# Another form of the feature map in a linear-attention block: three passes instead of four or five

## The chip, the cores and the metric

The kernel runs on one core of one Trainium2 chip. The time is the device time in microseconds (us), a median over several executions. The engines are named as the profile names them: PE (TensorE, matmuls), PEld (its weight loads), DVE (VectorE), ACT (ScalarE), POOL (GpSimd) and SP (SyncE, which here only issues DMAs). Each engine works through its own instructions in the order in which the program gives them; semaphores hold an instruction until what it needs is there. An instruction that waits holds up everything behind it on its engine.

## What is computed

One block of a network: layer norm, linear attention, a SwiGLU feed-forward network on the same normalised input, and a gated residual. There are 2048 tokens of width 1024, 32 heads of width 32, and a hidden width of 3584. All inputs are bfloat16.

```python
xn = _layernorm(x)
qkv = (xn @ wqkv) ...            # q, k, v per head
phi = lambda t: jnp.where(t > 0, t + 1, jnp.exp(t)) + 1e-6
pq, pk = phi(q), phi(k)
kv  = einsum("bhsd,bhse->bhde", pk, v)
z   = einsum("bhsd->bhd", pk)
num = einsum("bhqd,bhde->bhqe", pq, kv)
den = einsum("bhqd,bhd->bhq", pq, z)[..., None] + 1e-6
s   = (num / den) @ wo
g   = silu((silu(xn @ w_gate) * (xn @ w_up)) @ w_down)
out = x + s * g
```

The change concerns `phi`, the feature map, alone.

## The kernel before

**Phase 1, to about 128 us.** The 2048 tokens are 16 tiles of 128. For each tile `i` the kernel normalises the tile on DVE (L447, L448, L485), transposes it, and multiplies it by the K and V weights in four units of 512 columns (`c` = 0 to 3): eight matmuls each into a PSUM tile `kv_ps` (L528), of which there are three. Units 0 and 1 are K: `emit_Bev` sends them through the feature map into `pk_sb`, in bfloat16. Units 2 and 3 are V: ACT copies them to `v_sb` (L543). A tile later `emit_C` (L550) adds pk'v and the sum of pk to an accumulator `kvz`, which stays in PSUM.

**The Q projection, about 128 to 215 us.** The tokens are now four blocks `b` of 512. `emit_Q(b, g)` multiplies 128 columns (group `g` of 8) of Wq by a block: eight matmuls into a PSUM tile `q_ps` (L183), out of five such buffers, then the feature map into `pqT`. When `kvz` is complete, DVE masks it into `KVZ` (L662, L664). For each token tile of a block whose eight groups are done, `emit_ND` multiplies `pqT` by `KVZ`: eight matmuls into `nd` (L717). DVE then empties `nd`: it adds the epsilon to the denominators (L721), takes their reciprocals (L725) and writes the quotients to `o_blk` (L729, three instructions). There is one `nd` buffer. SP issues a DMA that transposes `o_blk` into `oT` (L738), and `emit_S` multiplies that by Wo (L748); ACT scales and stores the result (L751).

`run` (L865) sets the order: it takes a list of units, and after certain ones (`at`) puts in an `nd` item. For block 1 the list is eight Q units with an `nd` item of block 0 after every second; for blocks 2 and 3, Q units and S units alternate and an `nd` item follows every third unit. For blocks 1 and 2 an `nd` item also carries one step of weight preparation (`prep_step`).

**The feature map, `emit_phi`,** has three forms, all for 128 partitions by 512 columns:

- `in_place=False` (K of tiles 0 to 8): ACT Exp from PSUM into `e_t` (L154); ACT Relu from PSUM into `r_t` in SBUF (L161); DVE adds eps to `r_t` (L162); DVE takes min(e, 1) + r (L163). PSUM is free after the Relu.
- `in_place=True` (K of tiles 9 to 15, and groups 0, 1, 2, 4, 6 of Q block 0): ACT Exp (L154); DVE takes max(t, 0) + eps in PSUM (L157); DVE takes min(e, 1) + r with r in PSUM (L163).
- `act=True` (groups 3, 5, 7 of Q block 0 and all of blocks 1 to 3): ACT Relu(-t) into `e_t` (L148), ACT Exp(-that) in place (L149), ACT Relu(t) in PSUM (L150), then DVE adds the two and eps (L151). The DVE instruction isn't put in at once: it goes to the list `phi_late`, and `phi_flush` puts it in at the end of the step in `run`, that is behind the DVE work of an `nd` item that stands beside it.

`e_t` and `r_t` are float32, two buffers each.

**Beside all this** runs the preparation of the feed-forward weights: SP loads a weight tile, ACT sums its squares (L260), PE and DVE turn that into a power of two (L264, L269, L272, L273), DVE scales the tile in place (L283, 128 by 2048 bfloat16 in SBUF), POOL makes four difference tiles (L295 to L298), and the result is stored. From tile 8 of phase 1 on this goes on almost without a break. Before the attention's last stage POOL also makes sixteen difference tiles of Wo (L762). From about 246 us on the feed-forward network runs, in which PE is busy to the end.

Of the kernel before, what the change touches and what calls it, by code (L numbers as in the profile page):

```python
# [9 lines left out]
ACT = mybir.ActivationFunctionType  # L10
ALU = mybir.AluOpType
FP32 = mybir.dt.float32
BF16 = mybir.dt.bfloat16
# [8 lines left out]
def kernel(  # L22
# [11 lines left out]
    nc = tc.nc  # L34
    P = 128
# [10 lines left out]
    TB = min(512, S)  # L46
    NB = S // TB
    TPB = TB // P
    CW = min(512, D)
# [9 lines left out]
    EPS = 1e-6  # L59
# [58 lines left out]
    def xn_ap(dcs, tok):  # L118
        b = tok.start // TB
        return xn_blk_tiles[b][:, dcs, tok.start - b * TB:tok.stop - b * TB]  # L120
# [20 lines left out]
    def phi_flush():  # L141
        while phi_late:
            phi_late.pop(0)()

    def emit_phi(work, t_ps, dst, W, in_place=False, act=False):
        e_t = work.tile([P, W], FP32, name="e_t", tag="e_t")
        if act:
            nc.scalar.activation(out=e_t[:], in_=t_ps, func=ACT.Relu, scale=-1.0)  # L148
            nc.scalar.activation(out=e_t[:], in_=e_t[:], func=ACT.Exp, scale=-1.0)  # L149
            nc.scalar.activation(out=t_ps, in_=t_ps, func=ACT.Relu)  # L150
            phi_late.append(lambda: nc.vector.scalar_tensor_tensor(out=dst, in0=e_t[:], scalar=EPS, in1=t_ps,  # L151
                                                                   op0=ALU.add, op1=ALU.add))
            return
        nc.scalar.activation(out=e_t[:], in_=t_ps, func=ACT.Exp)  # L154
        if in_place:
            r = t_ps
            nc.vector.tensor_scalar(out=r, in0=t_ps, scalar1=0.0, scalar2=EPS, op0=ALU.max, op1=ALU.add)  # L157
        else:
            r_t = work.tile([P, W], FP32, name="r_t", tag="r_t")
            r = r_t[:]  # L160
            nc.scalar.activation(out=r, in_=t_ps, func=ACT.Relu)  # L161
            nc.vector.tensor_scalar(out=r, in0=r, scalar1=EPS, scalar2=None, op0=ALU.add)  # L162
        nc.vector.scalar_tensor_tensor(out=dst, in0=e_t[:], scalar=1.0, in1=r,  # L163
                                       op0=ALU.min, op1=ALU.add)


    blk12_es = ExitStack()
    blk12 = blk12_es.enter_context(tc.tile_pool(name="blk12", bufs=2, side="right", reuse_waits="tile"))
    phiw = p12.enter_context(tc.tile_pool(name="phiw", bufs=2, reuse_waits="tile"))
# [3 lines left out]
    def pqT_of(b):  # L173
        if b not in pqT_tiles:
            pqT_tiles[b] = blk12.tile([P, G, TB], BF16, name="pqT", tag="pqT")
        return pqT_tiles[b]

    def emit_Q(b, g, act=None):
        pqT = pqT_of(b)
        btok = slice(b * TB, (b + 1) * TB)  # L180
        q_ps = ps2.tile([P, TB], FP32, name="q_ps", tag="B2")
        for dc in range(DC):
            nc.tensor.matmul(q_ps[:], lhsT=wq_sb[:, dc, g * P:(g + 1) * P], rhs=xn_ap(dc, btok),  # L183
                             start=(dc == 0), stop=(dc == DC - 1))
        emit_phi(phiw, q_ps[:], pqT[:, g, :], TB, in_place=True, act=b > 0 if act is None else act)

    NPASS = NB // 2
    passes = list(range(NPASS - 1, -1, -1))
# [158 lines left out]
    def prep(n):  # L347
        for _ in range(n):
            prep_step()
# [13 lines left out]
    with ExitStack() as p1:  # L363
        wpool = p1.enter_context(tc.tile_pool(name="p1w", bufs=1, reuse_waits="tile"))
        work = p1.enter_context(tc.tile_pool(name="p1work", bufs=2, reuse_waits="tile"))
# [167 lines left out]
        def emit_Bev(i, c):  # L533
            kv_ps = kv_banks.pop((i, c))
            if i not in pkv_tiles:
                pk_sb = work.tile([P, D], BF16, name="pk_sb", tag="pk_sb")
                pkv_tiles[i] = (pk_sb, v_bufs[i % 2])
            pk_sb, v_sb = pkv_tiles[i]
            if c < NCC:
                emit_phi(phiw, kv_ps[:], pk_sb[:, c * CW:(c + 1) * CW], CW, in_place=i >= 9)  # L540
            else:
                vc = c - NCC
                nc.scalar.copy(out=v_sb[:, vc * GPC:(vc + 1) * GPC, 0:P],  # L543
                               in_=kv_ps[:].rearrange("p (g c) -> p g c", c=P))
# [29 lines left out]
        emit_TR(1)  # L574
        ln_pre(2)
        emit_Bev(0, 0)
        emit_Bmm(1, 0)
        emit_Bmm(0, 1)
        emit_Bev(1, 0)
        emit_N(2)  # L580
        emit_Bev(0, 1)
        emit_Bmm(1, 1)
        emit_Bmm(0, 2)
# [71 lines left out]
        ps2 = p12.enter_context(tc.tile_pool(name="ps2", bufs=5, space=PSUM, reuse_waits="tile"))  # L655
        stat_ps[0] = lambda: ps2.tile([P, 1], FP32, name="st_ps2", tag="B2")[:]
        emit_Q(0, 0)
        emit_C(NT - 1)
        for j in range(NJ):
# [3 lines left out]
                                    in1=mask[:, None, :].to_broadcast([P, ng, P]), op=ALU.mult)  # L663
            nc.vector.tensor_tensor(out=KVZ[:, g0:g0 + ng, P:P + HPG],  # L664
                                    in0=kvz_ps[:, j, 0:ng, P:P + 1].to_broadcast([P, ng, HPG]),
                                    in1=sel[:, None, :].to_broadcast([P, ng, HPG]), op=ALU.mult)
        for g in range(1, G):
            emit_Q(0, g, act=g in (3,5,7))
            if g in (2, 5):
                prep(1)  # L670
            phi_flush()
# [24 lines left out]
    with ExitStack() as p2:  # L696
        otp = p2.enter_context(tc.tile_pool(name="p2oT", bufs=2, reuse_waits="tile"))
        work = p2.enter_context(tc.tile_pool(name="p2work", bufs=4, reuse_waits="tile"))
# [137 lines left out]
        def q_item(b, g):  # L836
            return lambda: emit_Q(b, g)
# [597 lines left out]
```

## Time and profile before

| | |
|---|---|
| median of three runs | 758.13 us (757.99 to 758.14) |
| span of the profiled execution | 756.7 us |
| DVE L151, 27 times, 674 to 689 ns | Q, last step of the `act` form |
| DVE L157, 14 times on K and 5 on Q, 685 to 700 ns | max(t, 0) + eps in PSUM |
| DVE L162, 18 times, 373 to 454 ns | r + eps, float32 in SBUF |
| DVE L163, 37 times, 686 to 694 ns | min(e, 1) + r |
| ACT L148, L149, L150, 27 times each | medians 597, 630, 579 ns |
| ACT L154, 32 times on K and 5 on Q | medians 597 and 589 ns |
| ACT L161, 18 times | median 592 ns |
| DVE L283, 35 times, 747 to 3672 ns | median 755 ns |

The profile is of one execution. Its page gives each engine's busy time, the chain of work that ended last, and groups of equal instructions; the trace behind it can be asked for the order in time, for the waits, and for busy times by stretch. "Idle before" is the time that an engine stood still ahead of an instruction, and the releaser is what ended it. A time line gives the start in us from the span's beginning, the duration in us, engine, line and operation, what it writes and reads, and how many instructions are merged into the row.

### The profile page before, as it was taken

How to read it: one execution, taken by the hardware profiler on the slowest of the kernel's cores; microseconds unless marked ns; L12 is line 12 of the kernel's file. 1: busy time of each engine (PE TensorE's matmuls, PEld its weight loads, DVE VectorE, ACT ScalarE, POOL GpSimd, SP SyncE). 2: the span in 40 equal slices, each digit the busy share in tenths (PEclk: the TensorE clock that was granted, in tenths of full speed). 3: DMA queues.
4: the chain of work that ended last, by engine and by line, in shares of the span. 5: the costliest groups of instructions: out<-in, count | busy, mean ns of one | idle time of the engine just before them, and what ended most of it. 6: DMA issues, size and time to landing. Idle time of an engine off the chain costs nothing.

```text
span 756.7 us, 10426 instructions
## 1 busy us (share of the span) xinstructions
PE 746.6 (99%) x3662; PEld 349.0 (46%) x3731; DVE 558.5 (74%) x1031; ACT 376.3 (50%) x526; POOL 278.4 (37%) x352
## 2 busy tenths in 40 slices
PE   8999999999999999999999999999999999999997
PEld 4544544454454444444444444444444444444443
DVE  6687787896697788888889775368676777787335
ACT  5677776889956565666659311132322223211122
POOL 2444799998540276868585000100000000200000
PEclk9999999999999999999999999999999999999999
DMA  9968799879679668878799236398644445530824
GB/s 316 295 149 146 223 334 300 302 137 307 201 180 298 229 217 292 309 268 312 278 329 408 86 121 239 124 377 321 229 174 167 167 168 173 180 133 15 283 83 135
DMA packets 105845, 170.30 MB, mean 225 GB/s; under 512 B 34816, under 2 KB 82176, under 8 KB 95168
## 3 DMA queue, kind: packets, MB, share of 16 engines
q1 hardware_dynamic: 100144, 144.99, 59.3%
q0 software_dynamic: 4208, 22.15, 7.5%
q10 hardware_dynamic: 1440, 2.49, 0.9%
q8 instruction: 29, 0.48, 0.3%
q14 instruction: 24, 0.20, 0.1%
HBM read 111.67 MB, written 50.59 MB: 214 GB/s over the span
## 4 chain that ended last, share of the span: by engine, by line
PE 97%; DVE 1%; ACT 1%; issue 1%; ACTq 0%; DVEq 0%
PE zw L939 26%; PE kv_ps L528 15%; PE xb L939 13%; PE dzw L1124 12%; PE yb L939 6%; PE q_ps L183 6%; PE dx L1124 6%; PE dy L1124 3%; PE fx L790 3%; PE s_ps L748 2%; PE kvz L550 1%; PE nd L717 1%; PE df L1124 1%; PE warm_ps L564 1%; DVE w_sb L283 0%
## 5 line engine op out<-in xcount | busy, mean ns | idle before, releaser
L939 PEld LDWEIGHTS <-w_sb 128*128 128x128 f16 (+1 forms) x1568 | 152.1, 98 | 182.7
L939 PE MATMUL xb<-xnT,w_sb 128*128 128x512 bf16 x420 | 113.3, 379 | 1.5
L528 PE MATMUL kv_ps<-wkv_sb,xnT 128*128 128x512 bf16 x499 | 112.9, 379 | 1.1 <-DVE xnT L515 0.3
L939 PE MATMUL zw<-xnT,w_sb 128*128 128x512 bf16 x448 | 105.8, 379 | 0.0
L939 PE MATMUL zw<-S,w_sb 128*128 128x512 f16 x448 | 105.8, 379 | 0.0
L295 POOL TENSOR_TENSOR w_sb<-w_sb 128x512 f16<-128x512 bf16 x42 | 50.2, 1195 | 95.7 <-DVE w_sb L283 51.3
L260 ACT ACTIVATE w_sb<-w_sb 128x2048 bf16<-128x2048 bf16 x42 | 79.9, 1902 | 4.4 <-DMA w_sb<-in_B_w_up_dram 4.4
L1124 PE MATMUL dx<-w_sb,hT 128*128 128x512 bf16 x202 | 76.6, 379 | 0.3
L528 PEld LDWEIGHTS <-xnT 128*128 128x128 bf16 x512 | 48.4, 98 | 55.9 <-ACT xnT L517 0.8
L1124 PEld LDWEIGHTS <-hT 128*128 128x128 bf16 (+1 forms) x462 | 44.7, 98 | 52.4
L183 PE MATMUL q_ps<-xnT,wq_sb 128*128 128x512 bf16 x249 | 58.0, 379 | 0.4
L1015 ACT ACTIVATE sg<-cg 128x1024 bf16<-128x1024 f32 x28 | 29.6, 1057 | 57.4 <-DVE cg L1008 57.4
L939 PE MATMUL yb<-S,w_sb 128*128 128x512 f16 x224 | 57.4, 378 | 0.1
L1124 PE MATMUL dzw<-w_sb,hT 128*128 128x512 f16 (+1 forms) x190 | 57.0, 379 | 0.0
L1008 DVE SCALAR_TENSOR_TENSOR cg<-zw,rc_all,s 128x1024 f32<-128x1024 f32 x28 | 35.9, 1284 | 25.5 <-PE zw L939 13.8
L967 DVE SCALAR_TENSOR_TENSOR s<-yb,rc_all,s 128x512 f32<-128x512 f32 x42 | 31.5, 749 | 28.1 <-ACT s L966 28.1
L296 POOL TENSOR_TENSOR w_sb<-w_sb 128x512 f16<-128x512 bf16 x42 | 50.5, 1201 | 3.3
L1064 POOL TENSOR_TENSOR hs<-hT 128x512 f16<-128x512 bf16 x2 | 2.5, 1250 | 132.6 <-ACT sg L1015 132.6
L298 POOL TENSOR_TENSOR w_sb<-w_sb 128x512 f16<-128x512 bf16 x42 | 50.2, 1196 | 0.0
L297 POOL TENSOR_TENSOR w_sb<-w_sb 128x512 f16<-128x512 bf16 x42 | 50.2, 1195 | 0.0
L1098 POOL DMA_DIRECT2D out_dram<-io x16 | 8.7, 542 | 101.9 <-DVE io L1097 101.6
L966 ACT ACTIVATE s<-xb,rcl 128x512 f32<-128x512 f32 x14 | 9.6, 687 | 65.3 <-PE xb L939 65.3
(179 smaller groups left out, 1187.4 us busy)
## 6 DMA issues: line engine op xcount, KB each, us to landing
w_sb<-pk_g SPq DMA_DIRECT2D x27, 1024.0 KB, 6.3
pk_g<-w_sb SPq DMA_DIRECT2D x14, 1024.0 KB, 5.0
w_sb<-wd SPq DMA_DIRECT2D x14, 1024.0 KB, 6.0
w_sb<-pk_u SPq DMA_DIRECT2D x14, 1024.0 KB, 5.0
pk_u<-w_sb POOLq DMA_DIRECT2D x13, 1024.0 KB, 5.3
w_sb<-wd SPq DMA_DIRECT2D x14, 768.0 KB, 4.8
w_sb<-in_B_w_gate_dram SPq DMA_DIRECT2D x14, 512.0 KB, 6.7
w_sb<-in_B_w_down_dram SPq DMA_DIRECT2D x28, 256.0 KB, 4.9
```

The source lines that it names most:

```text
L183: nc.tensor.matmul(q_ps[:], lhsT=wq_sb[:, dc, g * P:(g + 1) * P], rhs=xn_ap(dc, btok), start=(dc == 0), stop=(dc == DC - 1))
L260: nc.scalar.activation(out=junk, in_=raw_view(key, t), func=ACT.Square, accum_out=asum[:])
L295: nc.gpsimd.tensor_tensor(out=T1, in0=b12, in1=b11, op=ALU.subtract)
L296: nc.gpsimd.tensor_tensor(out=T2, in0=b22, in1=T1, op=ALU.subtract)
L297: nc.gpsimd.tensor_tensor(out=T3, in0=b22, in1=b12, op=ALU.subtract)
L298: nc.gpsimd.tensor_tensor(out=T4, in0=b21, in1=T2, op=ALU.subtract)
L528: mm = nc.tensor.matmul(kv_ps[:], lhsT=xn_ap(dc, tok), rhs=wkv_sb[:, dc, c * CW:(c + 1) * CW], start=(dc == 0), stop=(dc == DC - 1))
L939: mm = nc.tensor.matmul(out, lhsT=lhs(k), rhs=rhs(k), start=(first and k == 0), stop=(k == HK - 1), skip_group_check=True)
L967: nc.vector.scalar_tensor_tensor(out=s2[:], in0=y_[:], scalar=rc, in1=s1[:], op0=ALU.mult, op1=ALU.add)
L1008: nc.vector.scalar_tensor_tensor(out=d12, in0=zw[:], scalar=rc, in1=s2[:, None, :].to_broadcast([P, 2, TB]), op0=ALU.mult, op1=ALU.add)
L1015: nc.scalar.activation(out=sg[:, 1:3, :], in_=cf[:], func=ACT.Silu)
L1124: nc.tensor.matmul(out, lhsT=lhs, rhs=rhs, start=first, stop=lastk, skip_group_check=True)
```

## The change

`emit_phi` is rewritten with the identity phi(t) = max(t + 1 + eps, min(exp t, 1) + eps): for t > 0 the first is larger, for t < 0 the second. It is one Exp on ACT from PSUM into `e_t`, now bfloat16; a clip on DVE in SBUF, in place, min(e, 1) + eps; and one DVE operation that reads PSUM and `e_t` and writes the result. `emit_Q` no longer chooses the `act` form, and K no longer chooses by tile. All 64 feature maps (32 of K, 32 of Q) take the same three steps, and both DVE steps of Q are now put in at once, inside `emit_Q`; `phi_late` stays empty. The `act` form remains in the code without being called.

```diff
-    def emit_phi(work, t_ps, dst, W, in_place=False, act=False):
-        e_t = work.tile([P, W], FP32, name="e_t", tag="e_t")
+    def emit_phi(work, t_ps, dst, W, act=False):
+        e_t = work.tile([P, W], FP32 if act else BF16, name="e_t", tag="e_t")
         if act:
...
         nc.scalar.activation(out=e_t[:], in_=t_ps, func=ACT.Exp)
-        if in_place:
-            r = t_ps
-            nc.vector.tensor_scalar(out=r, in0=t_ps, scalar1=0.0, scalar2=EPS, op0=ALU.max, op1=ALU.add)
-        else:
-            r_t = work.tile([P, W], FP32, name="r_t", tag="r_t")
-            r = r_t[:]
-            nc.scalar.activation(out=r, in_=t_ps, func=ACT.Relu)
-            nc.vector.tensor_scalar(out=r, in0=r, scalar1=EPS, scalar2=None, op0=ALU.add)
-        nc.vector.scalar_tensor_tensor(out=dst, in0=e_t[:], scalar=1.0, in1=r,
-                                       op0=ALU.min, op1=ALU.add)
-
+        nc.vector.tensor_scalar(out=e_t[:], in0=e_t[:], scalar1=1.0, scalar2=EPS, op0=ALU.min, op1=ALU.add)
+        nc.vector.scalar_tensor_tensor(out=dst, in0=t_ps, scalar=1.0 + EPS, in1=e_t[:], op0=ALU.add, op1=ALU.max)
...
-    def emit_Q(b, g, act=None):
+    def emit_Q(b, g, act=False):
...
-        emit_phi(phiw, q_ps[:], pqT[:, g, :], TB, in_place=True, act=b > 0 if act is None else act)
+        emit_phi(phiw, q_ps[:], pqT[:, g, :], TB, act=act)
...
-                emit_phi(phiw, kv_ps[:], pk_sb[:, c * CW:(c + 1) * CW], CW, in_place=i >= 9)
+                emit_phi(phiw, kv_ps[:], pk_sb[:, c * CW:(c + 1) * CW], CW)
...
-            emit_Q(0, g, act=g in (3,5,7))
+            emit_Q(0, g)
```

## The prediction

> **What bounds the kernel now.** I read the page's busy shares and its chain first.
>
> ```profile
> span 756.7 us, 10426 instructions
> PE 746.6 (99%) x3662; PEld 349.0 (46%) x3731; DVE 558.5 (74%) x1031; ACT 376.3 (50%) x526; POOL 278.4 (37%) x352
> PE 97%; DVE 1%; ACT 1%; issue 1%; ACTq 0%; DVEq 0%
> ```
>
> TensorE sets the end: 99% busy, 97% of the chain. ACT and DVE time counts only where PE waits for it. So I took the stretches of the feature map one by one (columns: stretch and length, then busy time of PE, PEld, DVE, ACT, POOL, then clock and DMA).
>
> ```profile
> 90.00:100.00 10.00, 9.95 (x57) 4.80 (x57) 8.27 (x15) 7.55 (x10) 9.84 (x9) 1.00 1.05 377
> ...
> 145.00:162.00 17.00, 16.85 (x106) 8.71 (x107) 14.06 (x35) 15.64 (x29) 16.92 (x16) 1.00 0.59 142
> 161.00:184.00 23.00, 22.57 (x131) 11.26 (x133) 20.13 (x47) 20.05 (x31) 20.09 (x19) 1.00 0.98 245
> ```
>
> The reader is to see three things: PE already loses nearly nothing here (0.15 us of 17); ACT is the fullest helper in 145 to 162; and POOL is busy without a break. Next, PE's order in time in the Q projection of block 1, where an nd group follows every second Q:
>
> ```profile
> 149.82 0.64 PE L717 MATMUL nd<-KVZ,pqT 128*128 128x132 bf16 x8
> 150.31 3.61 PE L183 MATMUL q_ps<-xnT,wq_sb 128*128 128x512 bf16 x16
> 153.76 0.63 PE L717 MATMUL nd<-KVZ,pqT 128*128 128x132 bf16 x8
> ...
> 157.68 0.63 PE L717 MATMUL nd<-KVZ,pqT 128*128 128x132 bf16 x8
> ```
>
> A pair (two Qs and one nd) takes PE 3.94 us (149.82 to 153.76, to 157.68). There is one nd buffer, so the next nd can't start until DVE has emptied the last one (L721, L725, L729). DVE's order in time:
>
> ```profile
> 154.01 0.69 DVE L151 SCALAR_TENSOR_TENSOR pqT<-e_t,q_ps 128x512 bf16<-128x512 f32 x1 [0.32 <-ACT q_ps L150]
> 154.61 0.37 DVE L721 TENSOR_SCALAR rden<-nd,rc_all 128x24 f32<-128x24 f32 x2
> 155.02 0.35 DVE L725 RECIPROCAL rden<-rden 128x32 f32<-128x32 f32 x1
> 155.41 1.35 DVE L729 TENSOR_TENSOR o_blk<-nd,rden 128x384 bf16<-128x384 f32 x3
> 156.68 0.68 DVE L151 SCALAR_TENSOR_TENSOR pqT<-e_t,q_ps 128x512 bf16<-128x512 f32 x1
> ```
>
> Emptying nd takes 156.68 - 154.61 = 2.07 us; with two L151 of 0.68 a pair costs DVE 3.43 of the 3.94 us.
>
> Last, from the time line of all engines, DVE's two-byte work in SBUF beside POOL:
>
> ```profile
> 137.13 1.73 DVE L283 TENSOR_SCALAR w_sb<-w_sb,cs_all 128x2048 bf16<-128x2048 bf16 x1
> 137.15 1.15 POOL L296 TENSOR_TENSOR w_sb<-w_sb 128x512 f16<-128x512 bf16 x1
> ...
> 138.26 1.60 POOL L297 TENSOR_TENSOR w_sb<-w_sb 128x512 f16<-128x512 bf16 x1
> ...
> 163.76 4.50 POOL L762 TENSOR_TENSOR To_sb<-wo_sb,To_sb 128x512 f16<-128x512 bf16 x4
> ...
> 165.13 3.67 DVE L283 TENSOR_SCALAR w_sb<-w_sb,cs_all 128x2048 bf16<-128x2048 bf16 x1
> ```
>
> Alone L283 takes 0.75 us. At 137.13 it took 1.73: it ended 0.55 us after L296 did, and the POOL operation behind it stretched from 1.15 to 1.60. At 165.13 it took 3.67 and ended 0.54 us after POOL's whole run (163.76 + 4.50). So such a DVE operation waits for POOL's running one and holds off the next. DVE operations that read PSUM show nothing of this: L151 stays at 674 to 689 ns throughout.
>
> **The change, part by part.** *ACT.* 18 Relus (L161, 0.592 us) go, 10.7 us; of 27 Q tiles two of three ACT passes go (L149 0.630, L150 0.579), 32.6 us. PE waited for ACT once in this region, 0.32 us at 173.22 with 0.39 more for its weight load, so about 0.4 comes back. One Exp into bf16 I leave at its 0.597 (the bf16 cast from PSUM, L543, is 0.586).
>
> *The clip, new on DVE, 64 times.* No such row exists. Nearest: L162 (512 wide, f32, SBUF, constants) 0.373 to 0.454; L485 at 512 columns bf16 0.410; L283 cut to 512 by L485's slope (0.545 at 1024, 0.410 at 512: 0.135 per 512), 0.754 - 3 x 0.135 = 0.35. Low end: L283 pro rata, 0.19. High end: L162's 0.45 plus a whole POOL operation of 1.15, 1.6. I take 0.35 alone, being bf16 in SBUF like L283, plus what the port adds.
>
> *The pass from PSUM* stays at L151's and L163's 0.68 to 0.69. For K tiles DVE gives up L162 (0.422) or L157 (0.696), for five Q tiles of block 0 L157 (0.694), so 18 tiles save 0.07, 19 save 0.35, and 27 Q tiles pay 0.35 more: 9.5 - 1.3 - 6.7 = +1.5 us before any wait. Spread evenly this would vanish in DVE's idle time; it isn't spread evenly.
>
> *The step that moves.* L151 of a Q used to be held back until after the nd work issued beside it. Now clip and pass stand ahead of that nd's L721, L725 and L729. If a clip waits, the whole emptying of nd waits behind it, and for that PE's next nd and the transposes into oT that SP issues.
>
> *Block 1 priced.* DVE per pair: 3.43 + 2 x 0.35 = 4.13 alone, 0.19 over PE's 3.94. POOL has no gap from 150.41 to 168.26, so each clip ends at a POOL boundary, and the pair becomes a whole number of POOL operations of 1.115 us (4.46 for four). Three (3.35) are fewer than the work; four are 4.46, plus two clips that each push POOL back by a quarter of 0.45 (0.11): 4.68. Four pairs ran from 145.61 to 161.62, 16.01 us: 4 x 4.68 - 16.0 = +2.7. Ends: with 0.19 per clip and no wait a pair is 3.81, hidden, 0; with 1.6 it is 6.63, +10.5.
>
> *Rest.* The period 161.62 to 167.30 still lies beside that POOL run with two clips: another +0.7. K tiles from 9 on and Q of block 0 (19 passes, POOL 98% busy) turn 1.38 us into 1.04 plus a wait of about 0.5 (22 L283 before 250 us average 1.223 against 0.754, 0.47 more): +0.16 each, 3 us more in some 60 us with 10 idle; through the three kv_ps banks I allow +0.5 (0 to 2). Blocks 2 and 3 after 176, where POOL has gaps: +0.3. POOL's own delay, 0.11 per clip, is covered: its last preparation ends at 212.8, phase 3 begins near 246.
>
> Sum: 2.7 + 0.7 + 0.5 + 0.3 - 0.4 = +3.8. From phase 3 on PE is full, and nothing there absorbs it. Profiled span 756.7 + 3.8 = 760.5; the runs' median lies 1.4 above that span, so 761.9, given as 762.0.
>
> *Two rules of the Trainium skill against the rows.* "SBUF — State Buffer" (SBUF: two separate sides) says the port pair that VectorE and GpSimd share is an exclusive lock held for a whole instruction. The rows at 137 agree; the one at 165.13 doesn't: two boundaries, at 166.0 and 167.1, went by without L283 getting in. By the rule a clip waits at most one operation, as I priced it; by that row up to four, which is the third rival below. "VectorE: DVE Perf Modes" (The TRN2 errata) gives 58 + FD/4 cycles at 0.96 GHz, 0.19 us for this clip as an estimate; by it alone a pair is 3.82 and block 1 costs nothing until the port adds 0.06 per clip.
>
> **The rivals.** *Hidden, no difference.* A clip this short slips in, or comes at 0.19 to 0.35: a pair is 3.8 to 4.13, 0 to +0.8 us in block 1, less 0.4 returned: 757.7 to 758.5. For: 2.9 idle us in 145 to 162 against 8 x 0.35 = 2.8. Against: POOL fills that stretch.
>
> *ACT was the limit, faster.* DVE's idle time before L151 ended with L150 (12.9 us in 10 waits), and ACT is 15.64 of 17. If the clip is 0.25 or less with its wait (break-even (3.94 - 3.43)/2), what remains is PE's lost time, at most some 2 us between 10 and 246: 756.1 to 757.7. Against: PE doesn't show more to give back.
>
> *Shut out.* As at 165.13, no clip enters POOL's sixteen operations (150.41 to 168.26). DVE then stands from about 151, PE stops at the second next nd, near 154, until 168.5: +14, 772. Against: at 137 and elsewhere the next boundary sufficed, and every entry breaks POOL's run anew.
>
> **How the numbers follow.** DVE paced by POOL's boundaries 66%, 759.7 to 768.5, likeliest 762.0; hidden 17%; ACT the limit 8%, of which 6 fall below 756.6; shut out 9%. This kernel's measurement tells 0.2% (1.5 us) from no change. Slower: 66 + 9 = 75%; within: 17 + 2 = 19%; faster: 6%. The range 757.2 to 768.5 holds the first two cases whole; the upper end is +10.4, the block 1 bound.
>
> **What would show it.** Right: the clips on DVE last 0.3 to 0.4 before 80 us and 0.6 or more between 90 and 168; nd groups in block 1 lie about 4.7 apart; PE's busy time falls short there by some 3 us; the first zw matmul is 4 us later; ACT is 43 us lighter to no gain. Wrong: clips of 0.35 amid a busy POOL, nd groups still 3.94 apart, or a PE wait that now ends with ACT or a K bank.

## The result, and the profile after

The changed kernel takes 763.23 us (762.96 to 763.48, four runs) against 758.13 us (four runs): ratio 1.0066, 95% interval 1.0051 to 1.0080. It is slower by 5.1 us. The profiled spans, 756.7 and 761.7 us, differ by 5.0.

The page after, with the lines that answer to those shown of before:

```profile
span 761.7 us, 10409 instructions
PE 746.9 (98%) x3662; PEld 348.5 (46%) x3731; DVE 567.5 (75%) x1058; ACT 339.0 (45%) x454; POOL 272.9 (36%) x352
PE 90%; DVE 5%; DMA 2%; issue 1%; ACT 1%; SPq 0%; POOL 0%; DVEq 0%; POOLq 0%; ACTq 0%
```

PE's busy time hardly moves (746.6 to 746.9), so PE does the same work and the five microseconds are time in which it waits. DVE's share of the chain goes from 1% to 5%. ACT is 37.3 us lighter, and the kernel is slower all the same. PE's waits after (who waited for whom: us in total, times, longest):

```profile
PE nd L708 <- DVE pqT L156: 1.7, 3, 0.9
PE nd L708 <- DVE o_blk L720: 1.7, 3, 0.8
```

Both stand at the nd groups: either the last `pqT` is late, or DVE hasn't emptied the one nd buffer. The busy times of the stretch around block 1 (columns as in the prediction: stretch and length, then PE, PEld, DVE, ACT, POOL, clock and DMA):

```profile
145.00:166.00 21.00, 17.59 (x102) 8.34 (x103) 20.38 (x45) 5.97 (x11) 20.92 (x19) 1.00 0.46 121
```

PE stands 3.4 of 21 us here, where before it lost 0.15 of 17. DVE is busy 20.38 of 21 us and POOL 20.92; ACT is busy 6. The time line of the changed kernel shows how one pair runs:

```profile
152.19 0.64 PE L708 MATMUL nd<-KVZ,pqT 128*128 128x132 bf16 x8 [0.77 <-DVE o_blk L720]
...
155.97 4.58 POOL L753 TENSOR_TENSOR To_sb<-wo_sb,To_sb 128x512 f16<-128x512 bf16 x4
...
156.59 0.68 DVE L155 TENSOR_SCALAR e_t<-e_t 128x512 bf16<-128x512 bf16 x1
...
156.73 0.64 PE L708 MATMUL nd<-KVZ,pqT 128*128 128x132 bf16 x8 [0.45 <-DVE o_blk L720]
...
157.91 0.52 DVE L155 TENSOR_SCALAR e_t<-e_t 128x512 bf16<-128x512 bf16 x1
...
159.07 0.37 DVE L712 TENSOR_SCALAR rden<-nd,rc_all 128x24 f32<-128x24 f32 x2
...
161.27 0.64 PE L708 MATMUL nd<-KVZ,pqT 128*128 128x132 bf16 x8 [0.45 <-DVE o_blk L720]
```

The nd groups are 4.54 us apart (152.19, 156.73, 161.27), where they were 3.94. POOL's four operations take 4.58, and the next four start 4.54 after these: a pair is exactly as long as four POOL operations. The two clips (L155) take 0.68 and 0.52. Elsewhere a clip can be shorter, or longer still (minimum, median, maximum in ns over all 64):

```profile
L155 DVE TENSOR_SCALAR e_t<-e_t x64: 241/416/1240, 12.2 to 218.3; 128x512 bf16<-128x512 bf16 x64
```

By stretch, from the clips' own records: 0.29 on average before 78 us, where POOL has only short operations; 0.80 from 78 to 128; 0.67 from 128 to 150; 0.60 beside POOL's Wo operations. A clip that meets a running POOL operation ends some 0.15 us after that operation does: at 156.59 it ended at 157.27, POOL's operation at 157.11. The POOL operation behind it lasts 1.20 instead of 1.15. Every clip that meets an operation of the weight preparation or of Wo ends so, and none waits for a second operation.

Where the 5.0 us arise, from the starts of PE's groups before and after: the first nd group comes 0.3 later (145.61, 145.90); the first pair after it takes 6.29 instead of 4.21 (+2.1); the next three 13.74 instead of 11.80 (+1.9); up to the Wo stage another 0.5 is added, with a wait of 0.8 inside the nd group that starts at 218.20. Phase 3 then starts at 249.25 instead of 244.43, another 0.2 is lost at its second group, and all of that reaches the end. The first pair, before (it ends at 149.82, shown in the prediction):

```profile
145.61 0.72 PE L717 MATMUL nd<-KVZ,pqT 128*128 128x132 bf16 x8
```

and after, with the late clips of block 0 that it waits for, beside POOL's weight preparation:

```profile
144.04 1.60 POOL L288 TENSOR_TENSOR w_sb<-w_sb 128x512 f16<-128x512 bf16 x1
144.55 1.24 DVE L155 TENSOR_SCALAR e_t<-e_t 128x512 bf16<-128x512 bf16 x1
...
145.90 0.51 PE L708 MATMUL nd<-KVZ,pqT 128*128 128x132 bf16 x6
146.43 0.52 DVE L155 TENSOR_SCALAR e_t<-e_t 128x512 bf16<-128x512 bf16 x1
...
146.57 0.23 PE L708 MATMUL nd<-KVZ,pqT 128*128 128x132 bf16 x1 [0.16 <-DVE pqT L156]
...
147.73 0.23 PE L708 MATMUL nd<-KVZ,pqT 128*128 128x132 bf16 x1 [0.93 <-DVE pqT L156]
```

The group ends at 147.96 instead of some 146.5, 1.4 late; the second group then comes another 0.9 late, waiting for `o_blk` (152.19, above).

### The profile page after: what moved, and what is told of

Its sections match the earlier page's. It is cut to its first block, busy times and chain, and to the rows that moved or that the text cites. A ratio compares the mean times of both kernels' runs of the same rounds, so it can differ in the third digit from the quotient of the medians.

```text
span 761.7 us, 10409 instructions
## 1 busy us (share of the span) xinstructions
PE 746.9 (98%) x3662; PEld 348.5 (46%) x3731; DVE 567.5 (75%) x1058; ACT 339.0 (45%) x454; POOL 272.9 (36%) x352
## 4 chain that ended last, share of the span: by engine, by line
PE 90%; DVE 5%; DMA 2%; issue 1%; ACT 1%; SPq 0%; POOL 0%; DVEq 0%; POOLq 0%; ACTq 0%
PE zw L930 25%; PE kv_ps L519 13%; PE xb L930 13%; PE dzw L1115 12%; PE yb L930 6%; PE dx L1115 6%; PE dy L1115 3%; PE fx L781 3%; PE q_ps L174 3%; PE s_ps L739 3%; DVE e_t L155 1%; DVE pqT L156 1%; DMA wkv_sb<-in_A_wqkv_dram 1%; DVE o_blk L720 1%; PE kvz L541 1%
## 5 line engine op out<-in xcount | busy, mean ns | idle before, releaser
L155 DVE TENSOR_SCALAR e_t<-e_t 128x512 bf16<-128x512 bf16 x64 | 32.9, 514 | 24.5 <-ACT e_t L154 24.5
```

The costliest lines, as they stand in the source:

```text
L155: nc.vector.tensor_scalar(out=e_t[:], in0=e_t[:], scalar1=1.0, scalar2=EPS, op0=ALU.min, op1=ALU.add)
```

## The experiments

The port theory: the clip works wholly in SBUF, so it waits for POOL's running operation, as L283 did at 137.13 in the kernel before; beside an unbroken POOL, that paces DVE and through the nd buffer PE.

**Q of blocks 1 to 3 in the old form.** `emit_phi_old` is `emit_phi` of the kernel before.

```diff
...
-        emit_phi(phiw, q_ps[:], pqT[:, g, :], TB, act=act)
+        if b > 0:
+            emit_phi_old(phiw, q_ps[:], pqT[:, g, :], TB, act=True)
+        else:
+            emit_phi(phiw, q_ps[:], pqT[:, g, :], TB)
```

> The changed kernel, with Q of blocks 1 to 3 in the old form (three ACT passes, one DVE pass held back); K and Q of block 0 keep the new one. Port theory (the clip in SBUF waits for POOL's running operation, and beside POOL's long run that paces the nd groups of block 1): the loss near 146 to 166 us goes, 758.0 to 758.8 us; nd groups 3.94 us apart. Rival, the K tiles carry the loss (three kv_ps banks freed later): 761 or more.

Measured: 759.34 us, ratio 1.0017 (1.0008 to 1.0026). After the first pair the nd groups are 3.92 to 3.95 apart again, as expected, and 3.9 us of the 5.1 are gone. This edit takes out the clips and the moved step together; later runs part them. The time is 0.5 above the expected span, because the first pair still takes 5.37: PE waits 1.4 us inside the first nd group for the last groups of block 0, whose clips stand beside POOL's weight preparation.

**K in the old forms.**

```diff
...
-                emit_phi(phiw, kv_ps[:], pk_sb[:, c * CW:(c + 1) * CW], CW)
+                emit_phi_old(phiw, kv_ps[:], pk_sb[:, c * CW:(c + 1) * CW], CW, in_place=i >= 9)
```

> The changed kernel, with K in the two old forms; all of Q keeps the new one. Port theory: nearly all of the loss stays, 762.4 to 763.4 us, nd groups of block 1 4.5 to 4.6 apart. Rival, K carries it: 760 or less.

Measured: 762.91 us, ratio 1.0064 (1.0049 to 1.0079), nd groups 4.55, 4.55 and 4.66 apart. So the loss stays without K's clips. The 0.3 us that this run is faster are not clear of the noise: the first nd group starts 0.36 earlier here (145.54, 145.90), and kernels whose code is the same up to that group start it up to 0.27 apart. But the one wait for a K bank in the changed kernel's trace (0.4 at 81 us) is gone here.

**The DVE steps of Q held back,** in blocks 1 to 3.

```diff
...
-        nc.vector.tensor_scalar(out=e_t[:], in0=e_t[:], scalar1=1.0, scalar2=EPS, op0=ALU.min, op1=ALU.add)
-        nc.vector.scalar_tensor_tensor(out=dst, in0=t_ps, scalar=1.0 + EPS, in1=e_t[:], op0=ALU.add, op1=ALU.max)
+        def two():
             nc.vector.tensor_scalar(out=e_t[:], in0=e_t[:], scalar1=1.0, scalar2=EPS, op0=ALU.min, op1=ALU.add)
             nc.vector.scalar_tensor_tensor(out=dst, in0=t_ps, scalar=1.0 + EPS, in1=e_t[:], op0=ALU.add, op1=ALU.max)
+        if late:
+            phi_late.append(two)
+        else:
+            two()
...
-        emit_phi(phiw, q_ps[:], pqT[:, g, :], TB, act=act)
+        emit_phi(phiw, q_ps[:], pqT[:, g, :], TB, act=act, late=b > 0)
```

> The changed kernel, with both DVE steps of Q in blocks 1 to 3 held back behind the nd work issued beside them, as the old form did. Port theory: two clips per pair still end at POOL boundaries, so nd groups stay 4.5 to 4.6 us apart and the time 762.3 to 763.4 us. Rival, the order (the emptying of nd starts too late because clip and pass stand ahead of it): groups back to 3.94, 760 us or less.

Measured: 761.75 us, ratio 1.0050 (1.0036 to 1.0064): outside both expectations. The groups behind the first pair are 4.31, 4.55 and 4.66 apart, so the pacing stays; but the first pair shrinks from 6.29 to 5.35, and 1.5 us come back in all. That is a balance: behind 217 us another 0.8 comes back (two periods take 3.33 and 3.06 instead of 3.85 and 3.34), and after 164.42 a period takes 6.48 instead of 5.67, since the nd group there now waits for a `pqT` held back. The order has a price of its own, which the theory as stated left out.

**POOL silent beside block 1.**

```diff
...
-        for o_, a_, b_ in ((To[0], bb[0][1], bb[0][0]), (To[1], bb[1][1], To[0]), (To[2], bb[1][1], bb[0][1]),
-                           (To[3], bb[1][0], To[1])):
-            for k in range(HG):
-                nc.gpsimd.tensor_tensor(out=o_[:, k], in0=a_[:, k], in1=b_[:, k], op=ALU.subtract)
+        To = [bb[0][0], bb[0][1], bb[1][0], bb[1][1]]
```

> The changed kernel without POOL's sixteen difference operations of Wo; what reads them takes slices of Wo instead, so the attention output is not the block's. POOL is then silent beside block 1. Port theory: clips there last 0.29 us, a pair costs DVE 2.07 + 2 x 0.69 + 2 x 0.29 = 4.03, nd groups 4.0 to 4.15 us apart, 760.2 to 761.3 us. Rival, the sheer amount of DVE work: groups stay at 4.5 or more and the time at 763.

Measured: 761.65 us, ratio 1.0048 (1.0034 to 1.0061). The time lines of PE and of DVE's clips in this kernel:

```profile
152.09 0.64 PE L708 MATMUL nd<-KVZ,pqT 128*128 128x132 bf16 x8 [0.77 <-DVE o_blk L720]
...
156.03 0.63 PE L708 MATMUL nd<-KVZ,pqT 128*128 128x132 bf16 x8
...
159.99 0.64 PE L708 MATMUL nd<-KVZ,pqT 128*128 128x132 bf16 x8
```

```profile
151.96 0.28 DVE L155 TENSOR_SCALAR e_t<-e_t 128x512 bf16<-128x512 bf16 x1
...
155.86 0.28 DVE L155 TENSOR_SCALAR e_t<-e_t 128x512 bf16<-128x512 bf16 x1
```

With the same DVE work but no POOL beside it, the groups are 3.94, 3.96 and 4.04 apart, and PE waits for none after the first. The clips there last 0.28 to 0.29. That rules out the amount of DVE work as the cause in these pairs. The expected 4.03 for DVE's pair was too much: it takes 3.90 here (151.96 to 155.86), under PE's 3.94, because rows that follow each other overlap (a pass of 0.69 is followed by the next row 0.61 after its start). The time is 0.35 above the expected span: the waits of 1.46 at 146 and 0.93 at 151 stay, since they arise beside the preparation and not beside the Wo operations.

**Shorter and longer POOL operations.** The same work of POOL, cut in other sizes:

```diff
-            for k in range(HG):
-                nc.gpsimd.tensor_tensor(out=o_[:, k], in0=a_[:, k], in1=b_[:, k], op=ALU.subtract)
+            for k in range(0, HG, 2):
+                nc.gpsimd.tensor_tensor(out=o_[:, k:k + 2], in0=a_[:, k:k + 2], in1=b_[:, k:k + 2], op=ALU.subtract)
```

This is the longer size; the shorter one puts two operations of 256 columns in the place of each.

> The changed kernel with each of POOL's sixteen Wo operations cut into two of 256 columns. Port theory: POOL's boundaries come about every 0.6 us instead of 1.11, so a pair is rounded up to a smaller step: nd groups of block 1 at 4.1 to 4.4 us instead of 4.55, clips there 0.3 to 0.5 us on average instead of 0.60, 761.8 to 762.7 us. Rival, a fixed price for working beside POOL whatever the length of its operations: groups stay at 4.55, 763.0 or more.

> The changed kernel with POOL's sixteen Wo operations joined two by two (eight of 1024 columns). The columns, the data and POOL's total work are the same. Port theory: boundaries every 2.2 us, so clips wait up to 2.3 us and a pair needs two or three whole operations: nd groups beside POOL's run 4.6 to 6.8 us apart, 764 to 770 us. Rival, a fixed price: no change, 763.2.

Measured with 256 columns: 763.07 us, ratio 1.0065 (1.0051 to 1.0079), groups 4.28, 4.49 and 4.60 apart, clips 0.28 to 0.66. The time is that of the rival, the first group that of the theory; by these figures the experiment doesn't decide. The reason lies in its sizes: POOL's half operations came 0.65 apart (eight in 5.24), and the pass between two clips takes 0.69, so a second clip just misses a boundary and waits for the next (0.66 each time). The trace says more. The half operations that the first clips of the four pairs met started at 151.50, 156.07, 160.55 and 165.04, each the seventh after the one before. The pair is rounded up here too; seven half operations (4.49) come to nearly the same as four whole ones (4.54).

Measured with 1024 columns: 768.77 us, ratio 1.0144 (1.0130 to 1.0158), 5.5 above the changed kernel. DVE's time line there:

```profile
154.19 1.49 DVE L155 TENSOR_SCALAR e_t<-e_t 128x512 bf16<-128x512 bf16 x1
...
158.38 1.50 DVE L155 TENSOR_SCALAR e_t<-e_t 128x512 bf16<-128x512 bf16 x1
```

and PE's:

```profile
152.04 0.64 PE L708 MATMUL nd<-KVZ,pqT 128*128 128x132 bf16 x8 [0.77 <-DVE o_blk L720]
...
158.52 0.64 PE L708 MATMUL nd<-KVZ,pqT 128*128 128x132 bf16 x8 [2.39 <-DVE o_blk L720]
...
164.85 0.64 PE L708 MATMUL nd<-KVZ,pqT 128*128 128x132 bf16 x8 [2.24 <-DVE o_blk L720]
```

The groups are 6.48 and 6.33 us apart, which is three operations of 2.1. POOL's work, DVE's and PE's are what they were; only the distance of POOL's boundaries has changed. With POOL silent at 3.94, this settles it: the pair is rounded up to POOL's boundaries.

**A clip with input and output of different width.**

```diff
-        nc.vector.tensor_scalar(out=e_t[:], in0=e_t[:], scalar1=1.0, scalar2=EPS, op0=ALU.min, op1=ALU.add)
+        m_t = work.tile([P, W], FP32, name="m_t", tag="r_t")
+        nc.vector.tensor_scalar(out=m_t[:], in0=e_t[:], scalar1=1.0, scalar2=EPS, op0=ALU.min, op1=ALU.add)
-        nc.vector.scalar_tensor_tensor(out=dst, in0=t_ps, scalar=1.0 + EPS, in1=e_t[:], op0=ALU.add, op1=ALU.max)
+        nc.vector.scalar_tensor_tensor(out=dst, in0=t_ps, scalar=1.0 + EPS, in1=m_t[:], op0=ALU.add, op1=ALU.max)
```

> The changed kernel with the clip reading bfloat16 and writing float32 into its own tile, so that its input and output differ in width. Port theory, if only DVE's faster modes in SBUF wait for POOL: the clip takes the 0.65 to 0.72 us of a plain pass everywhere, without the spread of 0.24 to 1.24; nd groups 2.07 + 4 x 0.69 = 4.83 us apart or a little more, 763.5 to 765.5 us. Rival, every DVE operation wholly in SBUF waits for POOL: clips above 0.8 beside POOL, groups at 5.5 or more, 766 or more.

Measured: 767.41 us, ratio 1.0122 (1.0109 to 1.0136). The premise fell: this clip takes 0.37 to 0.45 before 78 us, less than a plain pass, and up to 1.40 beside POOL. So it isn't a form that avoids the port, and whether a slower DVE operation wholly in SBUF would wait stays open. The groups are 4.80, 4.82 and 4.93 apart, near the theory's 4.83, though the clip isn't the plain pass that this figure was made of; the time lies in the rival's range. Neither expectation fits whole. Between 80 and 142 us PE also loses 2.3 us at K and Q banks, where the changed kernel loses 0.4.

**Two ACT passes and no clip,** from the kernel before: min(exp t, 1) is exp(-relu(-t)), so the old form loses its third ACT pass and DVE takes the maximum from PSUM.

```diff
-            nc.scalar.activation(out=t_ps, in_=t_ps, func=ACT.Relu)
-            phi_late.append(lambda: nc.vector.scalar_tensor_tensor(out=dst, in0=e_t[:], scalar=EPS, in1=t_ps,
-                                                                   op0=ALU.add, op1=ALU.add))
+            phi_late.append(lambda: nc.vector.scalar_tensor_tensor(out=dst, in0=t_ps, scalar=1.0 + EPS, in1=e_t[:],
+                                                                   op0=ALU.add, op1=ALU.max))
```

This form leaves out the epsilon where t is below 0.

> The kernel before, with its form of three ACT passes cut to two: Relu(-t), Exp, and then DVE takes max(t + 1 + eps, e) from PSUM, held back as before; no clip, nothing new in SBUF on DVE. All else is as before. Theory that PE is the limit and waited for ACT once (0.32 + 0.39 us): 757.3 to 758.0 us. Rival, ACT set the pace of the Q projection: below 757.

Measured: 757.38 us against 758.16 beside it, ratio 0.9990 (0.9981 to 0.9999): 0.8 us faster than before. The stretch of block 1:

```profile
145.00:166.00 21.00, 20.84 (x126) 10.80 (x128) 18.13 (x43) 15.12 (x24) 20.92 (x20) 1.00 0.64 161
```

POOL is as busy as in the changed kernel, DVE is at 18.1 of 21, and PE loses 0.16. The first group starts 0.35 earlier than before, which can be chance (the last run below, the same as before up to there, has it 0.27 earlier), and the first pair takes 3.92 instead of 4.21. PE's wait for ACT near 173 is gone, but the period around it is no shorter (5.96, before 5.94). No run here got more than this 0.8 from a lighter ACT.

**That form put in at once instead of held back.**

```diff
-            phi_late.append(lambda: nc.vector.scalar_tensor_tensor(out=dst, in0=t_ps, scalar=1.0 + EPS, in1=e_t[:],
-                                                                   op0=ALU.add, op1=ALU.max))
+            nc.vector.scalar_tensor_tensor(out=dst, in0=t_ps, scalar=1.0 + EPS, in1=e_t[:], op0=ALU.add, op1=ALU.max)
```

> e8_two_act with the DVE pass of Q put in at once, ahead of the nd work issued beside it, as the change does; no clip. It prices the order alone, which holding back the DVE steps (e3_late) put at about 1.4 us. If the order has its own price: first nd groups further apart than 3.94, 758.0 to 759.5 us. If the order only mattered because a clip stood there: 757.2 to 757.7.

Measured: 759.04 us against 758.31, ratio 1.0011 (1.0002 to 1.0020); the held-back form had 0.9990, so the order costs some 1.6 us (0.0021 of 758) without any clip. Pairs of 4.31 and 4.29 appear among those of 3.93, with PE waiting for `o_blk`:

```profile
149.40 0.64 PE L715 MATMUL nd<-KVZ,pqT 128*128 128x132 bf16 x8 [0.22 <-DVE o_blk L727]
...
157.62 0.64 PE L715 MATMUL nd<-KVZ,pqT 128*128 128x132 bf16 x8 [0.21 <-DVE o_blk L727]
```

Another 0.6 us is lost near 225. The sum is close to the 1.5 that holding back returned, though it arises at other places.

**Each form where it fits:** K before tile 9 in the changed form, K after it and all of Q by two ACT passes, Q held back.

```diff
...
+                emit_phi(phiw, kv_ps[:], pk_sb[:, c * CW:(c + 1) * CW], CW, act=i >= 9)
...
+        emit_phi(phiw, q_ps[:], pqT[:, g, :], TB, act=True, late=True)
```

> Three forms by what runs beside them: K of tiles 0 to 8, where POOL is nearly idle, in the changed form (one Exp, clip of 0.29 us, one pass); K of tiles 9 to 15 and all of Q by Relu(-t), Exp and one DVE pass from PSUM, held back for Q; so no clip beside a busy POOL. Port theory: no loss anywhere, and since e8_two_act left PE only some 0.7 us of waits there is little to win: 756.9 to 757.5 us. Rival, K in the changed form costs by itself (PSUM held longer): 757.8 or more.

Measured: 757.59 us against 758.31, ratio 0.9990 (0.9981 to 0.9999), like the last but one; the time lies between the two ranges expected. The clip costs nothing where POOL has only short operations: there it takes 0.24 to 0.31. It wins nothing there either, PE being full.

**One clip alone in POOL's run.** In the kernel before, a single Q tile in the changed form, held back.

```diff
...
+        if one:
+            nc.scalar.activation(out=e_t[:], in_=t_ps, func=ACT.Exp)
+            def two():
...
+            phi_late.append(two)
+            return
...
+        emit_phi(..., one=(b, g) == (1, 5))
```

> The kernel before with a single Q tile of 64 (block 1, group 5) in the changed form, its clip and pass held back like the old pass. The clip meets POOL's sixteen Wo operations some six to nine operations into their unbroken run, where nothing has broken it yet (the scaling at 165.13 in the kernel before was shut out to the run's end, while clips that met the run from its first operation on got in at every boundary). If a run is open at each boundary whenever it is met: the clip takes 0.4 to 1.3 us and the time stays within 0.3 of before, 757.6 to 758.4. If a run that nobody has broken early shuts DVE out to its end: the clip lasts until about 168, 7 to 12 us, PE stops for nd, and the time is 764 to 770.

Measured: 758.04 us, ratio 0.9998 (0.9989 to 1.0008). Its time line:

```profile
154.60 4.55 POOL L769 TENSOR_TENSOR To_sb<-wo_sb,To_sb 128x512 f16<-128x512 bf16 x4
...
156.41 0.62 DVE L150 TENSOR_SCALAR e_t<-e_t 128x512 bf16<-128x512 bf16 x1
...
163.56 4.95 POOL L769 TENSOR_TENSOR To_sb<-wo_sb,To_sb 128x512 f16<-128x512 bf16 x4
...
164.87 1.51 DVE L290 TENSOR_SCALAR w_sb<-w_sb,cs_all 128x2048 bf16<-128x2048 bf16 x1
```

The clip met POOL's sixth operation and got in at its end. More telling is the scaling at 164.87 (L283 of before): it takes 1.51 where it took 3.67, though nothing about it was changed. The run that it met had been broken once, at 157.

## Why the prediction was right, point by point

The mechanism, the place and the sign were right; the sum was +3.8 and the measurement +5.1. That the sum came so near owes something to luck: it left out 1.6 us in the first pair and had 0.7 for a period that lost nothing.

- **PE is the limit and ACT isn't.** Right. ACT got 37 us lighter (not 43: neighbouring rows overlap, as two Exps of 0.60 that take 1.07 together at 142.72) for no gain, and the best use of a lighter ACT found here gives 0.8 us.
- **The clip alone at 0.35.** It is 0.29. The estimate from the formula in the Trainium skill ("VectorE: DVE Perf Modes", The TRN2 errata) was 0.19; the same section says that the formula under-predicts the duration of a single operation. The shortest of 64 took 0.24, so rows of the same kernel were the nearer guide, and no run shows 0.19.
- **DVE's pair at 4.13, 0.19 over PE's.** Too much: with POOL silent it took 3.90, under PE's 3.94. The passes were added at 0.68 each, but the rows shown (154.01 to 154.61) put the next instruction 0.60 after a pass. The clips alone would have been hidden in these pairs; the rounding made the whole price of a pair.
- **The pair rounded to four POOL operations, 4.68.** Three of the four pairs took 4.54, 4.54 and 4.66. The push that a clip gives POOL is 0.05 instead of 0.11. Making the operations longer moved the pair to three of those, halving them, to seven of those; taking POOL away gave 3.94.
- **Four pairs at +2.7.** This is the term that was mis-sized: they cost +4.0 (145.90 to 165.93 is 20.03, against 16.01). The whole difference lies in the first pair, 6.29. Two things were left out of it. The last clips of block 0 stand beside the preparation (1.24 and 0.52 at 144.6 and 146.4), and PE waits 1.4 us for them inside the nd group. And the step that moves was described but given no price: holding the steps back takes 0.9 off the first pair and returns 1.5 in all, and putting them in at once without a clip costs 1.6.
- **The period after, +0.7.** Wrong: 5.67 against 5.68, and PE is busy 5.62 of it. The scaling that took 3.67 there before took 0.75 in the changed kernel, at 170.84, clear of the run; that DVE had this time for the clips is a likely reason, which no run tried by itself.
- **K at +0.5, later blocks at +0.3, ACT's waits at -0.4.** K's old forms gave back 0.3, not clear of the noise. What lies behind 171 comes to about +0.7 in all: a wait of 0.8 for `pqT` in the nd group of 218.20, less 0.3 that two shorter periods give back, and 0.2 early in phase 3. So small terms were about right and partly for other reasons.
- **The Trainium skill's rule of the exclusive port** ("SBUF — State Buffer", SBUF: two separate sides). The clips agree with it: each waited for the operation it met and no longer, ending 0.15 us after it in the changed kernel. The row at 165.13 in the kernel before doesn't agree, nor does the same scaling in four other kernels (last section).
- **The rivals.** Hidden: no, 2.9 idle us in DVE's stretch don't help when each clip is twice its length and the pair is rounded up; with POOL silent it came true for the pairs behind the first. ACT the limit: no. Shut out: no clip was, in any run; each got into POOL's Wo operations at the first boundary after it had asked.

## What to carry to other kernels

Moving a step from ACT to a short DVE operation in SBUF costs what POOL is doing at that moment: price it by the length of POOL's operations, not by its own. In this loop, with one buffer between two engines, the period became a whole number of those operations, so DVE work that fitted with POOL silent (3.90 of 3.94 us) cost 0.6 a pair. Where a step is also moved ahead of the one that empties the buffer, price the order separately; here it was nearly a third of the loss. The cheaper way here was one more pass on ACT, which had time for it, and a DVE operation that reads PSUM.

## What the runs showed that was not expected

A long POOL run can shut a DVE operation out for several POOL operations. The scaling of 128 by 2048, which elsewhere waits for one operation at most (up to 1.76 us), took 3.67 in the kernel before, 3.22 with Q of blocks 1 to 3 in the old form, 4.15 with two ACT passes, 3.88 with each form where it fits and 2.12 with two ACT passes put in at once. Each time one to three boundaries went by, and it ended 0.55 us after the end of the sixteen operations. Where a clip had broken the run seven operations earlier, the same instruction took 1.51; it met the fourteenth operation, as it did in the kernel with each form where it fits. But that clip itself got in at the first boundary, though nothing had broken the run before it. Why the boundaries are closed in a long run isn't shown; that it is the run's unbroken length is an inference from these six kernels and wasn't tried by itself.
